# A new stored order and new engine choices for the same pieces of an attention and spatial-gate kernel

## The chip, the cores and the metric

The kernel runs on one core of one Trainium2 chip. The core has a matrix engine (TensorE, "PE" in the profile, with its weight loads as "PEld"), three engines for elementwise work (VectorE "DVE", ScalarE "ACT", GpSimd "POOL"), a queue engine that issues DMAs (SyncE "SP") and 16 DMA engines. Each engine runs its own instructions in their order and waits on semaphores for the others. The metric is the device time of one execution in microseconds, the median of several runs.

## The reference

Batch 8, 8 heads, 576 positions, head size 64. Two attentions are added: one over positions pooled by 4, one over a band of 7 positions. Their sum x, with the heads joined, goes through a gated MLP whose gate mixes positions.

```python
q_d = q.reshape(B, H, Sd, factor, D).mean(axis=3)      # k_d, v_d likewise
out_up = np.repeat(sm_attn(q_d, k_d, v_d), factor, axis=2)
mask = np.abs(pos[:, None] - pos[None, :]) < factor
out_local = softmax(np.where(mask, scale * q @ k.T, -1e9)) @ v
x = out_up + out_local                                  # (8, 576, 512)
h = gelu_tanh(x @ w_in)                                 # 512 -> 1024
u, v = h[..., :512], h[..., 512:]
v_n = (v - mu) / np.sqrt(var + 1e-06) * g_ln            # over the last axis
v_s = np.einsum('ts,bsd->btd', w_sg, v_n) + b_sg[None, :, None]
out = x + (u * v_s) @ w_out
```

## The kernel before

The work is 32 groups g = 0 to 31 (a batch and a pair of heads; four groups make a batch) and 8 MLPs (a batch each). All of it is cut into 2105 named pieces ("tasks"), each on one engine. Nothing is scheduled on the way: the string ORDER (lines 88 to 195) lists the names, and `place` (line 64) and the last loop of the kernel emit the pieces one after another in that order. A name may carry an engine (`/V` VectorE, `/A` ScalarE, `/P` GpSimd, `/S` SyncE); otherwise its piece has one engine. So ORDER sets the sequence of every engine's instructions, SyncE's loads among them, and also which buffer a piece gets: a pool of 8 PSUM banks, 10 buffers "X" and 38 buffers "R" are handed out first freed, first taken.

```python
for word in ORDER.split():
    name, _, e = word.partition("/")
    t = named.pop(name)
    for k in t.takes:
        where[k] = free[k[0]].pop(0)
    for k in t.gives:
        readers[k] -= 1
        if not readers[k]:
            free[k[0]].append(where[k])
    order.append((t, e or next(iter(t.engines))))
```

The names, with the group or the batch and piece as number:

- Loads on SP: lq, lk (q and k of a group, 293 KB each), lv (v in groups of four, for the pooled attention), lw (v in windows), w.. (weights), small and b (constants). os stores a quarter of a batch's output.
- qs, ks: pooled sums of q and k (line 391 on VectorE, 394 and 395 on GpSimd); vs the same of v, on GpSimd, from group 4 on.
- S and Y, or YS: scores of the band and of the pooled attention on TensorE (lines 417, 424, 445). Groups 0 to 3 have them as two pieces.
- ma, mb, mx, my, nx, ny: mask, row maxima and biases. ea, eb, ec: exponentials on ScalarE (lines 484, 492). re, rc: sums and reciprocals. np, nq: the normalization of both (lines 506, 509).
- T, U, t: transposes of the probabilities on TensorE (lines 512, 521). pa, pb, pc, pe: their evacuation from PSUM (line 221).
- D: probabilities by v on TensorE (lines 573, 589). oe, od, xa, xb: upsampling and sum of both attentions, on VectorE for the most part. xh, xl, xc: x split into a high and a low part.
- v (vk in batch 0, where the piece is cut in four): x by the half of w_in that is gated by position (line 691, 512 columns). vg, va, vj: GELU. vb, vp, vn: layer norm. vh, vl: high and low part.
- u, ua: the other half of w_in (line 769) and its GELU on ScalarE (line 788).
- s: the spatial product (line 769); sa, sm: bias (line 807) and gate (line 814); gh, gl: high and low part.
- o (ok in batch 7): w_out (line 769); oa adds x (line 843).
- wu, wq, wb, wt, wh, wl: the weights, which come as 64-bit numbers, are turned into a high and a low float32 part (lines 299 to 326).

Weights and activations stand in two parts each, and three products of the parts are added, so v, u, s and o are runs of 8 to 14 matmuls of 288 or 512 columns ("wide" work). S, Y, YS and D are many matmuls of at most 64 x 64 weights, several of them in different quarters of the array at a time. A YS leaves 56 matmul records in the trace, a D 56 (104 in groups 0 to 3), each with a weight load.

Of the kernel before, what the change touches and what calls it, by code (L numbers as in the profile page):

```python
# [98 lines left out]
od3 xa3 xb3 vk0.2 ea5 xc2 vk3.2 T4 wtr2 wlz1/V eb5 xh3/A re5/V rc5 nq5/P wq3 t4 np5/P U4 vk4.2 vk2.2 wq2 pa4/A xl3/V  # L99
v0.0 xc3 lq8 wuz0 wqr1/A ks6/V wtz0 wbr1 pb4/V pc4/V pe4/A v0.2 vg0.2 vb0.2 wq0 lk7 ks7/V vg0.0 vb0.0 v0.3 vg0.3 wr3  # L100
lw4 wtr1 v0.1 vg0.1 whz0/A wlz0/P v0.4 va0.4/A whz3/A whq3/A vj0.4 vg0.4 whq0/A vp0.2 wlz3/P whr2/A YS6 ma6 mb6 my6
wlq0/P D4 lq7 vb0.1 vp0.1 T5 pa5/A vp0.0 oe4/A od4 lw6 ks8/V qs7/P whq2/A vn0.2 u0.0 xa4 u0.1 ua0.0 ua0.1 vn0.1 vb0.4
vp0.4 lv5 u0.4 ua0.4 wur3 wq4 vh0.1/A whq4/A vh0.2/A wqr0/A wur0 u0.5 ua0.5 U5 vn0.0 mx6 vb0.3 xb4 wlq3/P vh0.0/A
pb5/A vn0.4 u0.6 vp0.3 vn0.3 wlr2/V whq1/A wlq1/V pc5/A ua0.6 vh0.3/A t5 pe5/A wqr3/A lq9 lk10 vh0.4/A u0.2 ua0.2 u0.3
vl0.2/V vl0.0/V ny6/A wlq4/V wlq2/V vl0.1/V lv6 lq15 lw5 nx6/V qs8/V YS7 ma7 ua0.3 u0.7 ua0.7 vl0.3/P vl0.4/V mb7 wbr0
vs6 vs5 mx7 s0.1 sa0.1 ea6 sm0.1/P lk11 my7 eb6 lq13 lw8 ny7/A ec6 s0.0 sa0.0 sm0.0/V wbr3 wtr3 s0.3 re6/V sa0.3
sm0.3/P wtr0 s0.2 sa0.2 xh4/A rc6 np6/V nx7/A ec7 qs9/V YS8 gh0.0/A gl0.0/V ma8 mb8 mx8 eb7 sm0.2/V nq6/P whr3/A
wlr3/P D5 oe5/A T6 pa6/A gh0.1/A ea7 s0.5 sa0.5 lw7 sm0.5/P lk9 ks9/V s0.4 sa0.4 od5 my8 ny8/V gl0.1/V s0.6 t6 U6
re7/A whr1/A pb6/A lq10 s0.7 lw13 lv8 lw9 sm0.4/P sa0.6 lq14 lk14 gh0.2/A pc6/A pe6/A nx8/V xa5 rc7 ec8 sa0.7 sm0.7/V
sm0.6/P YS9 xb5 wlr1/P D6 ea8 gh0.3/A whr0/V gl0.2/P gl0.3/V o0.6 o0.7 my9 oe6/V ma9 mb9 od6 xa6 xb6 eb8 mx9 re8/A rc8  # L110
xh5/A o0.4 xl5/V oa0.4 lv7 lq12 lq11 wlr0/P o0.0 oa0.0 ks10/P np7/P T7 xh6/A ny9/A nq7/P U7 pa7/V pb7/V pc7/A t7 pe7/V
oa0.6 oa0.7 o0.1 oa0.1 os0.0 nx9/A ea9 ec9 qs10/P YS10 my10 ny10/A eb9 re9/A vs7 D7 oe7/V od7 ma10 mb10 mx10 nx10/A
eb10 qs11/V xa7 rc9 xb7 xh7/V np8/P T8 lk12 lv13 nq8/P o0.2 t8 xl4/P xl6/P xc6 oa0.2 xl7/P lv9 ks11/V o0.3 pa8/V U8
pb8/A ea10 ec10 re10/V rc10 v1.1 vg1.1 vb1.1 v1.0 pc8/A vg1.0 YS11 pe8/V vs8 D8 oa0.3 ma11 mb11 mx11 nq9/P xc7 nq10/P
np9/P U9 oe8/V nx11/V ea11 T9 pa9/V od8 vb1.0 xa8 eb11 lw12 lk13 my11 v1.2 u1.4 ny11/A vg1.2 pb9/V pc9/A vs9 o0.5
np10/P vb1.2 vp1.0 vn1.0 vh1.0/V T10 lv10 ks12/P qs12/P xc5 xc4 vl1.0/V vp1.1 vn1.1 vp1.2 ua1.4 vn1.2 t9 pe9/A U10
ec11 re11/V v1.4 va1.4/A vj1.4 vg1.4 xb8 pa10/V pb10/A vb1.4 u1.2 ua1.2 v1.3 vg1.3 rc11 vh1.2/V lk16 YS12 my12 os0.1
ma12 oa0.5 mb12 D9 vb1.3 oe9/V t10 ny12/V ec12 lw11 lw10 os0.2 nq11/P vp1.4 od9 xa9 xb9 np11/P mx12 u1.5 ua1.5 vp1.3
vn1.3 pc10/V pe10/V vs10 ks13/P os0.3 vh1.3/A vh1.1/A u1.6 ua1.6 qs13/V vl1.2/V u1.7 ua1.7 u1.3 ua1.3 D10 vn1.4
vh1.4/V vl1.4/P vl1.1/P lq19 lv11 YS13 ma13 mb13 nx12/A ea12 vl1.3/P ks14/V my13 oe10/V eb12 T11 lv12 vs12 vs11 U11  # L120
u1.0 od10 xa10 xb10 mx13 xh10/A xl10/P nx13/A ny13/A pa11/A eb13 pb11/A s1.1 sa1.1 t11 pc11/A ec13 pe11/A s1.3 re12/V
rc12 nq12/V np12/V s1.0 sa1.0 qs14/P ua1.0 u1.1 ua1.1 s1.2 YS14 ma14 mb14 mx14 xh8/A xh9/A xl9/P nx14/V eb14 sm1.0/P
sa1.2 sm1.2/P D11 oe11/V sm1.1/V sa1.3 gh1.0/A sm1.3/V T12 od11 pa12/V s1.7 my14 ny14/A ea14 s1.5 sa1.5 xa11 xb11 s1.4
lv14 xc10 t12 sm1.5/P xl8/V ea13 xh11/V sa1.7 xl11/V xc11 vs13 U12 pb12/A pc12/V s1.6 re13/A rc13 np13/V v2.0 ks16/P
v2.3 gl1.0/P xc9 ec14 re14/A rc14 vg2.0 lk15 ks15/V T13 sm1.7/V nq13/V np14/P pa13/V U13 pb13/A pe12/A vg2.3 pc13/V
t13 u2.4 ua2.4 gh1.1/A qs15/V lk19 sa1.4 YS15 ma15 mb15 D12 pe13/V T14 u2.5 my15 ny15/A ec15 oe12/V gl1.1/V v2.1 vg2.1
pa14/V mx15 sm1.4/P sa1.6 sm1.6/P nx15/V vb2.0 lq16 qs16/V gh1.3/V vp2.0 vn2.0 gl1.3/V od12 xa12 xb12 gh1.2/A gl1.2/P
v2.2 vg2.2 u2.2 vb2.3 vp2.3 xc8 vb2.1 vp2.1 YS16 ma16 mb16 D13 oe13/V nq14/V vn2.3 eb15 ea15 ua2.2 re15/A rc15 nq15/P
# [5 lines left out]
eb17 od15 xa15 xb15 xh15/A xl15/P ua2.1 lv17 lk18 my17 ks18/V s2.0 sa2.0 sm2.0/V sa2.1 lq18 qs18/P ny17/V sm2.1/V u2.6
s2.2 sa2.2 lv16 sm2.2/V ua2.6 xh12/A ea17 lk21 u2.7 xl13/P xc13 s2.3 sa2.3 sm2.3/V vs16 s2.5 sa2.5 ec17 sm2.5/V s2.6
xl12/P lk23 xh14/A xl14/P ua2.7 s2.4 gh2.1/A sa2.4 sm2.4/V sa2.6 sm2.6/P U16 YS18 ma18 mb18 mx18 T16 pa16/V t16
gh2.2/A xc15 gl2.2/P my18 ny18/V ec18 s2.7 sa2.7 sm2.7/V lk20 pb16/V pc16/V re17/A gh2.3/A v3.0 u3.0 ua3.0 vg3.0 vb3.0
pe16/A v3.1 vg3.1 lw21 gl2.3/P gl2.1/P v3.2 os1.1 nx18/V rc17 nq17/P vp3.0 np17/V gh2.0/A vg3.2 vb3.1 YS19 my19 ma19
mb19 mx19 D16 eb18 ea18 oe16/A od16 xa16 re18/V rc18 gl2.0/P vs17 T17 pa17/A U17 pb17/V pc17/A v3.3 vg3.3 vp3.1 u3.5
nq18/P vb3.2 o2.6 xb16 oa2.6 o2.2 oa2.2 o2.0 vn3.1 vh3.1/A vn3.0 t17 np18/P T18 pa18/A u3.4 vb3.3 o2.3 vp3.2 oa2.3  # L140
pe17/V vn3.2 vp3.3 ua3.4 nx19/A ea19 o2.1 ks20/V lw17 os2.1 vh3.0/V lq20 vn3.3 oa2.0 oa2.1 qs20/V xc14 xc12 v3.4
va3.4/V o2.4 oa2.4 o2.7 oa2.7 U18 o2.5 ny19/A ua3.5 ec19 u3.6 pb18/V vj3.4 vg3.4 vb3.4 pc18/V oa2.5 YS20 ma20 my20 D17
t18 ua3.6 vp3.4 vn3.4 vh3.4/V u3.1 vl3.0/V u3.2 mb20 vh3.2/A pe18/V lw18 mx20 vl3.2/V qs21/V vh3.3/A lk22 ny20/A eb19
# [845 lines left out]
```

## Time and profile before

| | us |
|---|---|
| median of 3 runs | 574.63 |
| lowest and highest run | 574.22, 578.1 |
| the profiled execution | 574.64 |
| its span, first to last instruction | 572.9 |
| busy: TensorE matmuls, weight loads | 552.4, 517.2 |
| busy: VectorE, ScalarE, GpSimd | 407.7, 356.6, 320.8 |

The granted TensorE clock is 1.000 in the whole span. TensorE's matmuls are 6992 and cover 96% of the span, but "busy" counts from a matmul's start to its modelled end, and consecutive matmuls overlap; how far apart they start tells their cost better. The three elementwise engines are idle 29% to 44% of the time. The loads (52.64 MB read in all) come mostly in the first tenth of the span, when the weights are read and prepared too. Instruction fetches are DMAs as well; the page has them as queues of kind "instruction". In a list of waits, "issue" stands where an engine was idle and the profile shows nothing that it waited for.

### The profile page before, as it was taken

How to read it: one execution, taken by the hardware profiler on the slowest of the kernel's cores; microseconds unless marked ns; L12 is line 12 of the kernel's file. 1: busy time of each engine (PE TensorE's matmuls, PEld its weight loads, DVE VectorE, ACT ScalarE, POOL GpSimd, SP SyncE). 2: the span in 40 equal slices, each digit the busy share in tenths (PEclk: the TensorE clock that was granted, in tenths of full speed). 3: DMA queues.
4: the chain of work that ended last, by engine and by line, in shares of the span. 5: the costliest groups of instructions: out<-in, count | busy, mean ns of one | idle time of the engine just before them, and what ended most of it. 6: DMA issues, size and time to landing. Idle time of an engine off the chain costs nothing. (4 is left out here: it accounts for less than half of the span.)

```text
span 572.9 us, 17455 instructions
## 1 busy us (share of the span) xinstructions
PE 552.4 (96%) x6992; PEld 517.2 (90%) x6992; DVE 407.7 (71%) x912; ACT 356.6 (62%) x1236; POOL 320.8 (56%) x403
## 2 busy tenths in 40 slices
PE   5689999999999999999998999999999999999997
...
GB/s 312 299 305 363 60 242 154 115 81 153 78 61 23 122 107 150 88 2 67 203 107 94 105 63 262 26 120 25 1 108 141 57 15 53 2 1 1 64 1 185
DMA packets 30609, 63.21 MB, mean 110 GB/s; under 512 B 3520, under 2 KB 3776, under 8 KB 30528
## 3 DMA queue, kind: packets, MB, share of 16 engines
...
q8 instruction: 55, 0.90, 0.7%
q10 hardware_dynamic: 144, 0.30, 0.1%
...
HBM read 52.64 MB, written 9.44 MB: 108 GB/s over the span
## 5 line engine op out<-in xcount | busy, mean ns | idle before, releaser
L769 PE MATMUL ps<-wsg_h,R 128*128 128x288 f32 x576 | 121.4, 298 | 0.1
L769 PE MATMUL ps<-X,weight_z 128*128 128x288 f32 x512 | 109.0, 297 | 0.5 <-ACT pd L492 0.5
L769 PE MATMUL ps<-R,weight_r 128*128 128x288 f32 x768 | 107.4, 296 | 0.0
L769 PEld LDWEIGHTS ps<-R,weight_r 128*128 128x128 f32 x768 | 103.1, 188 | 0.5 <-ACT R L788 0.2
L691 PE MATMUL ps<-weight_y,X 128*128 128x512 f32 x320 | 97.8, 399 | 0.0
L484 ACT ACTIVATE X<-X,nb 128x64 f32<-128x64 f32 x280 | 93.6, 339 | 5.7 <-DVE nb L463 5.4
L769 PEld LDWEIGHTS ps<-wsg_h,R 128*128 128x128 f32 x576 | 93.9, 188 | 0.6 <-issue 0.4
L769 PE MATMUL ps<-wsg_l,R 128*128 128x288 f32 x320 | 92.5, 295 | 0.0
L769 PEld LDWEIGHTS ps<-X,weight_z 128*128 128x128 f32 x512 | 84.2, 188 | 1.5 <-ACT pd L492 0.7
L769 PE MATMUL ps<-R,weight_z 128*128 128x288 f32 x256 | 75.5, 295 | 0.0
L691 PEld LDWEIGHTS ps<-weight_y,X 128*128 128x128 f32 x320 | 57.9, 188 | 11.3
L769 PEld LDWEIGHTS ps<-wsg_l,R 128*128 128x128 f32 x320 | 60.2, 188 | 0.0
L807 DVE SCALAR_TENSOR_TENSOR vs<-ps,small_sb,b_sb 128x288 f32<-128x288 f32 x64 | 32.5, 512 | 38.1 <-PE ps L769 35.4
L814 POOL TENSOR_TENSOR R<-R,vs 128x288 f32<-128x288 f32 x34 | 28.6, 848 | 54.7 <-DVE vs L807 30.4
L221 ACT COPY R<-ps 112x192 f32<-112x192 f32 (+4 forms) x74 | 28.1, 395 | 45.8 <-PE ps L512 14.4
L732 POOL TENSOR_TENSOR rs<-rs,nhalf 128x1 f32<-128x1 f32 (+1 forms) x40 | 23.9, 599 | 56.7 <-DVE rs L723 54.3
L484 ACT ACTIVATION_READ_ACCUMULATOR X<-X,nb 128x1 f32 x280 | 53.3, 190 | 0.0
L221 ACT CAST R<-R 128x576 fp32r<-128x576 f32 (+2 forms) x46 | 29.5, 648 | 36.0 <-DVE R L814 15.1
L691 PE MATMUL ps<-weight_y,R 128*128 128x512 f32 x128 | 50.5, 394 | 0.0
L843 DVE TENSOR_TENSOR R<-ps,R 128x288 f32<-128x288 f32 x64 | 27.8, 450 | 30.2 <-PE ps L769 30.2
L760 POOL TENSOR_TENSOR R<-R,R 128x512 fp32r<-128x512 f32 (+1 forms) x24 | 32.2, 1349 | 30.0 <-DVE R L221 14.9
L769 PEld LDWEIGHTS ps<-R,weight_z 128*128 128x128 f32 x256 | 48.2, 188 | 0.7
...
## 6 DMA issues: line engine op xcount, KB each, us to landing
...
```

The source lines that it names most:

```text
L221: (nc.scalar.copy if e == "A" else ENG[e].tensor_copy)(**kw)
L484: nc.scalar.activation(out=st["ms"][:, t, :], in_=src, func=AF.Exp, bias=st["nb"][:, t:t + 1], scale=scale, accum_out=sums[par][:, t:t + 1])
L691: nc.tensor.matmul(out=acc, lhsT=r32(l), rhs=r32(weights[f"y{k}"][:, 0, w]), start=(i == 0 and ks[0] == 0), stop=(i == len(ops) - 1 and ks ...
L732: nc.gpsimd.tensor_tensor(out=rs[0:n], in0=rs[0:n], in1=nhalf[0:n], op=ALU.pow)
L760: ENG[e].tensor_tensor(out=r32(dst), in0=vact[s][0][0:n], in1=vh[0:n, 0:DM], op=ALU.subtract)
L769: nc.tensor.matmul(out=acc[:, 0:HALF], lhsT=r32(l), rhs=r32(r), start=(first and n == 0), stop=(last and n == len(ops) - 1))
L807: nc.vector.scalar_tensor_tensor(out=vsb[i], in0=at["ps", "m", b, "s", i][:, 0:HALF], scalar=g_sb[:, i // 2:i // 2 + 1], in1=b_sb[:, half( ...
L814: ENG[e].tensor_tensor(out=u[:, half(i)], in0=u[:, half(i)], in1=vsb[i], op=ALU.mult)
L843: nc.vector.tensor_tensor(out=x[:, half(i)], in0=at["ps", "m", b, "o", i][:, 0:HALF], in1=x[:, half(i)], op=ALU.add)
```

## The change

Only the string ORDER is replaced. It holds the same 2105 names. Their sequence is new on every engine and on SP's queue, and where a piece may run on one of two engines the choice differs for some: of the evacuations pa, pb, pc, pe 88 of 128 are now on ScalarE (68 before), of oe 19 of 32 (10 before); of gh 15 of 32 are on VectorE (8), of xh 18 of 32 (10), of sm 39 of 64 (30), the rest of sm being on GpSimd; qs and ks move between VectorE and GpSimd, with GpSimd's share of the two going from 26 to 29 of 64. No piece changes what it computes, and the pools keep their sizes. Cut to the start, the places where YS and D pieces stand side by side, and the end:

```diff
-lk0/A lq0/S ks0/P qs0/V Y0 my0 ny0/V ec0 small wy1 lq1/S qs1/P wqy1/V wby1 wuy1 wy0 wuy0 wqy0/A S0 mx0 lk1/S S1 ks1/P
-wby0 nx0/A ea0 eb0 re0/A mx1 lq2 qs2/V wty1 lk2 wz1 wuz1 wty0 ks2/P Y1 my1 nx1/V rc0 ea1 ny1/V S2 ec1 mx2 np0/P wy3
-wqy3/V nq0/V T0 why0/V wly0/P t0 U0 pa0/V pb0/V pc0/V pe0/V Y2 my2 wqz1/V nx2/A eb1 re1/V why1/V rc1 np1/P nq1/P lk4
-lw0/S lv0/S wz2 lq4 wbz1 wuz2 wqz2/A D0 wby3 ny2/A lk6 lq3 ea2 oe0/V od0 xa0 ks4/V qs3/V lk3 wuy3 lv1/S wty3 wly1/P
-qs4/P T1 eb2 ks3/P xb0 pa1/V wtz1 lw1/S S3 mx3 ec2 re2/A rc2 xh0/A why3/A nq2/V nx3/A U1 ea3 YS4 ma4 lv3 mb4 wy2 t1
-pb1/A my4 pc1/V pe1/A eb3 Y3 my3 ny3/A ec3 ny4/A wbz2 whz1/V xl0/P xc0 D1 t2 mx4 lv2 np2/P T2 re3/A U2 oe1/V wqy2/A
-pa2/A wtz2 vk3.0 rc3 nq3/P np3/P ec4 od1 xa1 xb1 xh1/A vk0.0 lk5 ks5/V pb2/V vk1.0 lq5 qs5/V pc2/A pe2/A wby2 YS5 wz3
-whz2/A lw2 xl1/P xc1 wr0 wr1 nx4/A vk0.1 vk3.1 wuy2 wq1 ma5 mb5 mx5 my5 D2 wqz3/A wbz3 ea4 wty2 why2/A eb4 ny5/A lv4
-oe2/V od2 xa2 wz0 xb2 vk1.1 T3 wr2 wur1 nx5/A lw3 re4/V U3 pa3/A pb3/A wlz2/P wly3/P pc3/V lq6 xh2/A wuz3 rc4 xl2/V t3
-pe3/V vk2.0 wly2/P vk4.0 vs4 nq4/P np4/P vk2.1 wqz0/A wbz0 vk1.2 lk8 qs6/V vk4.1 ec5 wtz3 b wur2 wqr2/A wbr2 D3 oe3/V
...
-pb14/V os1.2 vl2.0/P lq21 lw15 os1.3 vh2.1/A vl2.1/P ea16 vn2.4 u2.3 ua2.3 u2.0 ua2.0 qs17/V os1.0 vh2.4/V pc14/V YS17
-ma17 qs19/P pe14/A re16/A D14 mb17 mx17 oe14/A od14 vl2.4/V xa14 xb14 rc16 nq16/V D15 ks19/V oe15/V np16/V s2.1 nx17/A
...
-s3.5 YS21 T19 t19 re20/V my21 sa3.5 ma21 ny21/A rc20 U19 ec21 s3.7 pa19/V pb19/V pc19/A pe19/A ks22/V YS22 os2.3 D18
-oe18/A sm3.5/V gl3.1/P np20/P gh3.2/V gl3.2/P sa3.7 sm3.7/P ma22 mb22 lw19 D19 mb21 nq20/V T20 mx21 pa20/V od18 oe19/V
...
-oa3.3 va4.4/A vj4.4 u4.6 ua4.6 u4.4 ua4.4 vp4.1 vn4.1 vh4.1/V vl4.0/P YS23 my23 vl4.1/P ny23/V ma23 mb23 vg4.4 vb4.4
-mx23 vp4.4 D20 oe20/V ec23 D21 od20 oe21/V od21 xa20 U22 pb22/V xb20 xa21 xb21 u4.7 vs22 nx23/A ea23 eb23 u4.1 ua4.1
...
-s7.5 sa7.5 o6.7 sm7.5/P gh7.2/A s7.6 s7.7 sa7.7 sm7.7/V sa7.6 sm7.6/V oa6.6 oa6.7 os6.3 os4.3 os6.0 os6.2 gl7.2/P ok3
-ok2 ok1 ok0 gh7.3/A gl7.3/V o7.2 oa7.2 o7.3 oa7.3 os7.1 o7.0 oa7.0 o7.1 oa7.1 o7.4 oa7.4 o7.6 oa7.6 os7.3.0 os6.1 o7.5
-oa7.5 os7.2 os7.0 o7.7 oa7.7 os7.3.1
+lk0/A lq0/S ks0/V qs0/V Y0 my0 ny0/A small S0 ec0 wy1 wuy1 lq1/S qs1/P wqy1/V wby1 wty1 mx0 wy0 lk1/S S1 ks1/P wqy0/A
+wby0 lk2 ks2/V mx1 lq2 qs2/P lq3 Y1 S2 my1 wuy0 wy3 wqy3/V nx0/A ea0 eb0 re0/V rc0 qs3/P ny1/V nx1/A ea1 wby3 mx2 ec1
+np0/P T0 nq0/P pa0/V U0 pb0/V pc0/V t0 pe0/V wz1 Y2 wty0 lk3 why1/V wqz1/V eb1 re1/V rc1 lk5 nq1/P wuz1 nx2/V ea2
+lw0/S lv0/S D0 oe0/A eb2 my2 ny2/V lq5 wbz1 np1/P U1 T1 why0/V wly0/P ks3/V od0 xa0 ec2 lk4 ks4/V t1 pa1/A pb1/A wuy3
+lw1/S lq4 qs4/V wtz1 whz1/V wlz1/P wz2 pc1/A pe1/V Y3 my3 wy2 wqz2/A xb0 re2/A rc2 np2/P S3 mx3 ny3/A ec3 qs5/V lv1/S
+wz3 nx3/A ea3 YS4 my4 ma4 ny4/A nq2/P wty3 wly1/P mb4 T2 pa2/A eb3 ks5/V wbz2 xh0/V U2 pb2/A xl0/P re3/A rc3 nq3/P lw2
+pc2/V np3/P t2 pe2/A lv2 lv3 D1 oe1/V od1 xc0 xa1 YS5 ma5 mb5 xb1 wuz2 wtz2 lv4 wqy2/A ec4 wqz3/A vk0.0 vk2.0 wby2 T3
+wuy2 wty2 my5 why3/A pa3/A xh1/A U3 pb3/A t3 wuz3 mx4 xl1/V nx4/V wly3/V ny5/A pc3/A pe3/V wr0 ec5 D2 oe2/A vs4 wz0
+wbz3 xc1 lk6 od2 xa2 xb2 mx5 vk2.1 wq0 lw3 lw8 wq4 xh2/V eb4 vk1.0 whz2/A ea4 re4/V vk4.0 vk3.0 vk1.1 wtz3 whz3/A
+why2/V whq0/A wuz0 wqz0/A vk4.1 vk0.1 nx5/A eb5 wly2/V wr2 D3 xl2/V vk1.2 vk2.2 vk0.2 xc2 wr1 lq6 rc4 nq4/P np4/P wq3
+vk3.1 ks6/V lq7 oe3/V od3 xa3 xb3 wlz3/V xh3/V ea5 re5/A xl3/P xc3 wlq0/P vk4.2 vk3.2 T4 wbz0 wtz0 U4 whq4/A t4 wlq4/V
+v0.0 v0.2 rc5 qs6/V wqr2/A pa4/A wbr2 nq5/P wq2 lw4 vg0.0 vb0.0 v0.4 vp0.0 lw5 wlz2/P pb4/A lw13 qs7/V pc4/A va0.4/A
+vj0.4 b wq1 pe4/A v0.1 whz0/A vg0.1 vb0.1 vp0.1 u0.6 vn0.0 wlz0/P lv6 wr3 wqr0/A v0.3 whq3/A vg0.3 vb0.3 vg0.2 vg0.4
...
+vl1.1/P pc11/V pe11/V vp1.2 vn1.2 ua1.7 u1.1 ua1.4 ua1.5 vh1.2/V ks13/P YS13 my13 ma13 mb13 vl1.4/V lq14 D11 D10
...
+vb2.0 pb13/V pc13/V t13 pe13/V lk16 ks16/V YS15 pe12/A vp2.0 my15 ma15 ny15/V ec15 lv14 D12 oe12/V od12 mb15 mx15
+nx15/A vb2.2 eb15 D13 oe13/V xa12 od13 vp2.2 vs14 os0.3 v2.4 va2.4/A o1.6 rc14 o1.2 o1.0 ea15 vn2.2 oa1.6 vn2.0
...
+sa2.3 xb14 u2.7 lq21 lw21 s2.4 ua2.7 lw17 os1.2 sm2.2/P sa2.4 sm2.4/V mx17 sm2.3/V s2.5 sa2.5 YS18 ma18 mb18 my18 D15
+oe15/A od15 nx17/A xh14/V eb17 xa15 xb15 U16 t16 s2.7 ea17 sm2.5/P qs19/P xc12 sa2.7 xh15/V xl14/P xl15/V v3.0 vg3.0
...
+pa28/A YS30 ma30 os4.2 os4.3 sm5.7/P gh5.3/V gl5.3/P D26 oe26/A od26 xa26 gl5.2/V xb26 xh26/V xl26/P D27 oe27/A U28
...
+oa5.1 t29 pe29/V eb30 YS31 ma31 D28 vs30 vn6.3 mb31 mx31 os5.1 os5.0 nx31/A eb31 oe28/V od28 vn6.2 vh6.2/V xa28 D29
...
+sm7.3/P gh7.1/A gl7.1/P s7.7 sa7.5 sm7.5/V s7.4 sa7.4 sm7.4/V s7.6 sa7.6 sa7.7 sm7.6/V gh7.2/V gl7.0/P o6.0 u7.7 ua7.7
+gl7.2/V ok2 ok0 sm7.7/V gh7.3/V gl7.3/V ok1 o7.0 oa7.0 o7.2 oa7.2 oa6.0 oa6.1 os6.1 o7.6 ok3 oa7.6 os5.2 os6.0 o7.1
+oa7.1 o7.4 o7.5 os7.0 os7.3.0 oa7.4 oa7.5 os7.2 o7.3 oa7.3 os7.1 o7.7 oa7.7 os7.3.1
```

More of the change, by code (lines that the diff above doesn't have):

```diff
@@ L99 @@
[L99 to L128, printed above, removed]
@@ L134 @@
[L134 to L143, printed above, removed]
@@ L174 @@
-pc28/A D26 oe26/V od26 ea29 D27 oe27/A gh5.3/V gl5.3/P xl24/P xa26 xb26 YS30 my30 ma30 t28 ny30/A ec30 od27 xh26/V
-xa27 xb27 xh27/A xl26/P xl27/V o5.2 o5.3 mb30 mx30 lv28 qs31/V nx30/V lk31 ks31/V v6.0 re29/A pe28/A rc29 nq29/V vg6.0
-vb6.0 np29/P vs29 eb30 vs28 v6.2 vg6.2 vb6.2 u6.0 ua6.0 v6.1 oa5.2 oa5.3 os5.1 xc27 T29 U29 pa29/A vp6.2 vn6.2 pb29/A
-pc29/V D28 vg6.1 YS31 ma31 mb31 vh6.2/A vl6.2/P ea30 re30/A vp6.0 vn6.0 vh6.0/V vb6.1 t29 pe29/V v6.3 vg6.3 u6.1 ua6.1
-lw29 D29 oe28/V od28 oe29/A u6.6 ua6.6 mx31 xc25 od29 xc24 xa29 vp6.1 vn6.1 my31 nx31/A ny31/A vl6.0/P xc26 vb6.3 v6.4
```

121 lines of the change are left out of this document (81 added, 40 removed).

## The prediction

> **What bounds the kernel.** I read the page's busy shares and slices first, then a table by stage, then TensorE's waits by stage, then the timeline at each pause.
>
> ```profile
> span 572.9 us, 17455 instructions
> PE 552.4 (96%) x6992; PEld 517.2 (90%) x6992; DVE 407.7 (71%) x912; ACT 356.6 (62%) x1236; POOL 320.8 (56%) x403
> PE   5689999999999999999998999999999999999997
> q8 instruction: 55, 0.90, 0.7%
> ```
> ```profile
> core 0: us, PE busy (x) PEld busy (x) DVE busy (x) ACT busy (x) POOL busy (x), PEclk, DMA share, GB/s
> 299.91:302.17 2.26, 2.26 (x140) 2.26 (x136) 1.83 (x6) 0.29 (x1) 2.09 (x2) 1.00 0.91 252
> 338.22:340.48 2.26, 2.26 (x141) 2.26 (x137) 1.82 (x6) 1.55 (x3) 1.26 (x1) 1.00 0.06 10
> 213.36:216.08 2.72, 2.72 (x144) 2.66 (x134) 2.19 (x5) 0.76 (x4) 2.53 (x4) 1.00 0.10 23
> 39.60:45.70 6.10, 5.93 (x132) 4.90 (x127) 5.34 (x13) 5.57 (x26) 5.79 (x6) 1.00 1.04 311
> 6.10:62.20 56.10, 48.71 (x991) 38.82 (x991) 49.20 (x112) 50.38 (x211) 44.10 (x48) 1.00 0.96 306
> 62.20:569.50 507.30, 503.67 (x6004) 478.36 (x6002) 356.89 (x797) 306.22 (x1026) 274.47 (x347) 1.00 0.28 87
> 569.50:572.90 3.40, 0.00 (x0) 0.00 (x0) 0.42 (x1) 0.00 (x0) 0.00 (x0) 1.00 0.50 184
> ```
>
> TensorE is the bound. From 62.2 us on it is idle 507.30 - 503.67 = 3.6 us; in the start (6.1 to 62.2) 56.10 - 48.71 = 7.4 us; 6.1 us lie before its first matmul and 3.4 behind its last. The matmuls are the same in both kernels, so an order can win only from these, and from what TensorE pays when it changes between kinds of work.
>
> ```profile
> PE ps L589 <- issue: 2.6, 2, 1.8
> PE ps L769 <- ACT pd L492: 0.5, 1, 0.5
> PE ps L445 <- ACT R L788: 0.3, 1, 0.3
> ...
> PEld ps L445 <- issue: 1.8, 10, 0.4
> ```
> ```profile
> 46.85 0.35 PE L521 MATMUL ps<-small_sb,pd 112*112 112x112 f32 x2 [0.90 <-PE ps L521]
> 216.49 0.30 PEld L769 LDWEIGHTS ps<-wsg_h,R 128*128 128x128 f32 x2 [0.36 <-issue]
> 304.16 0.57 PE L589 MATMUL ps<-R,X 64*64 64x58 f32 x24 [1.77 <-issue]
> 341.55 0.57 PE L589 MATMUL ps<-R,X 64*64 64x58 f32 x23 [0.86 <-issue]
> ```
>
> Of the 3.6 us idle after the start, 2.6 are two pauses in which no engine is waited for. They are instruction fetches. Queue q8 moved 55 pieces of 0.90 MB / 55 = 16 KB, and TensorE issued 2 x 6992 = 13984 instructions: 254 a piece. Counted from TensorE's first instruction, waits included, the four pauses above stand at numbers 1473, 6337, 8385 and 9153: each is 193 above a multiple of 256. The block ahead of each was used up in 2.26, 2.26, 2.72 and 6.10 us (rows above; 140 + 136 of them, less those that lie over an edge). From a block's first instruction to the first of the next, pause included, it took 304.16 - 299.91 = 4.25, 341.55 - 338.22 = 3.33, 216.49 - 213.36 = 3.13, and with the loads at 311 GB/s 46.85 - 39.60 = 7.25 us. I read this as: the next block is asked for when one is entered, arrives 3.1 to 4.25 us later (up to 7.25 under the loads of the start), and TensorE stops if the block is used up sooner. Only bursts of small matmuls do that: YS (56 matmul records), a late D (56), an early D (104). Here are YS22 D18 D19, YS23 D20 D21 and YS17 D14 D15.
>
> [...]
>
> **The change, part by part.** Only the string ORDER differs: each engine's sequence and some choices of engine; the 415 TensorE tasks are the same.
>
> *Late fetch pauses.* Three D/YS in a row stand in the new order four times: YS13 D11 D10, YS15 D12 D13, YS30 D26 D27, YS31 D28 D29. With two instructions a matmul and the waits spread as before, the block edge falls 220, 124, 179 and 125 instructions into bursts of about 340. So a block holds at most 220 instructions of a burst and at least 36 of wide work. Wide matmuls go every 0.13 us:
>
> ```profile
> 299.00 0.29 PE L769 MATMUL ps<-wsg_l,R 128*128 128x288 f32 x1
> ...
> 299.13 0.30 PE L769 MATMUL ps<-wsg_h,R 128*128 128x288 f32 x1
> ```
>
> The shortest block then lasts 2.26 x 220/276 + 18 x 0.13 = 4.1 us, near the upper turnaround of 4.25, and before it the queue could run ahead through the wide work. I take no pause. Gain: 1.77 + 0.86 + 0.36 = **-3.0 us**. If the waits are spread otherwise the edges move by a dozen instructions, which leaves that.
>
> *The start.* I walked the new lists of the five queues by hand to the end of v0.3 (the last v of batch 0), each task at its duration in the trace, starting when its engine is free and its inputs are there.
>
> ```profile
> 4.80 0.75 DVE L391 TENSOR_REDUCE qd<-R 128x144 f32<-128x576 f32 x1 [3.60 <-DMA R<-in_qT_dram]
> ...
> 4.96 0.66 POOL L394 TENSOR_TENSOR half<-R 128x288 f32<-128x288 f32 x1 [3.28 <-DMA R<-in_kT_dram]
> ...
> 6.19 1.33 PE L445 MATMUL ps<-kd,qd 64*64 64x144 f32 x16 [6.19 <-POOL kd L395]
> ...
> 8.51 1.28 ACT L492 ACT_TABLE_LOAD   x1 [8.51 <-DVE nbd L475]
> ...
> 16.67 1.26 POOL L506 TENSOR_TENSOR X<-X,rc 128x640 f32<-128x640 f32 x1
> ...
> 17.98 0.64 PE L512 MATMUL ps<-small_sb,X 122*128 122x122 f32 x4 [2.00 <-POOL X L506]
> ...
> 35.73 0.91 POOL L509 TENSOR_TENSOR pd<-pd,rc 128x432 f32<-128x432 f32 x1
> ...
> 37.82 1.42 POOL L608 TENSOR_TENSOR R<-R,X 128x576 fp32r<-128x576 f32 x1
> ```
>
> ks0 goes to VectorE ahead of qs0: 4.96 + 0.66 + 0.75 = 6.4, Y0 0.2 later. ny0 goes to ScalarE ahead of ec0: 0.2 later; if the table loaded for it isn't that of exp, 1.28 more. Then np0 (1.26) starts at 16.9 to 17.4 instead of 16.67, because re0 and rc0 now stand behind wqy3 on VectorE: T0 at 18.2 to 18.7 instead of 17.98. U1 and T1 wait for np1 until 24.4 to 25.0. But t1 and Y3 follow without the old gaps, and YS4 is done at 29.5 to 30.0, with the same work behind it that was done at 31.45. T2 then waits for np2 until 31.8 to 32.4. T3 waits for GpSimd, which has xl0, nq3 and np3 in a row from 36.0: 1.42 + 0.91 + 1.26, so 39.6 to 40.2; t3 is done at 40.6 to 41.1, against 40.1 for the same work before. From there D2, D3 and the v pieces find their inputs, and v0.3 ends at 59.6 to 60.2. Before, TensorE began u0.0 at 62.2, with YS6, D4 and T5 behind it (2.65 us) but u0.6 (1.6) not; that makes 61.1. So 0.9 to 1.5 sooner, the old pause at 46.85 counted in. On SP's queue lq3, lk3 and lk5 go ahead of lv0 in place of lk4: two loads of 0.3 MB, 1.9 us at 311 GB/s. D0, which waited for evacuations and not for lv0, is itself 0.5 to 1 us later; if lv0 ended last, about 1 us is lost there.
>
> Against that stand the new order's own pauses in the start. D1 and YS5 are now next to each other, with the edge 78 instructions into D1: that block (130 instructions of D1, YS5, vk0.0) takes some 3.4 us. Turnaround there: 5.8 to 7.25. The pause is 2.4 to 3.9, but T3 has 2 us of its own waiting behind it, so 1.3 net, and 0.4 for the next block (5.9 us). Bounds: 0 (the fetch is early) to 5.2 (3.9 + 1.3, nothing absorbed). Sum for the start: -1.2 + 1.7 = **+0.5**.
>
> *Changes between kinds of work.* From wide work to a burst: 27 before, 21 after; from transposes (T, U, t) to a burst 8 and 12; transpose to other transpose 37 and 45; burst to anything else 36 and 34. None costs over 0.18 us (1.8 over 10, in the row of TensorE's weight-load waits above); by the start-to-start times of each kind, -0.5 + 0.6 + 0.6 - 0.3 = **+0.4**.
>
> *Engine choices.* 20 evacuations (pa to pe) more on ScalarE, 9 sm from GpSimd to VectorE, 7 gh from ScalarE to VectorE, 10 changes of ScalarE's table fewer (56 to 46).
>
> ```profile
> L814 POOL TENSOR_TENSOR R<-R,vs 128x288 f32<-128x288 f32 x34 | 28.6, 848 | 54.7 <-DVE vs L807 30.4
> ...
> L484 ACT ACT_TABLE_LOAD x18 | 23.1, 1283 | 0.3
> ```
>
> GpSimd loses about 14 us, ScalarE 10 x 1.28 = 13, VectorE stays. All are idle at least 28% of the time, and TensorE's queue covers them: **0**. Without that cover a place costs what one late operation does, 0.5 to 0.85. Known old waits in the later part are 0.5 + 0.3; I find some six more close places in the new order than in the old (D15 stands 2.4 us ahead of v3.0, with od15, xa15, xb15, sa2.7, xh15, xl15 between on VectorE), most covered because the late operand comes last in the accumulation: **+0.3**, from -0.8 to +4.
>
> *The end.* Behind s7.6 come o6.0, u7.7, ok2, ok0, ok1 (51 wide matmuls at 0.13, 6.6 us) while VectorE finishes gl7.2 and gl7.3; last are o7.7, its add and a half store as before: 3.4 us stay. **0**.
>
> Sum, against the profiled execution's 574.64 (span 572.9 and 1.7 around it; the median of the runs is 574.63): 574.6 - 3.0 + 0.5 + 0.4 + 0.3 = **572.8**, say 572.6.
>
> **The rivals.**
> *Faster still.* The walk is too careful about the start; half of its 7.4 us of idle time goes and the early fetch is hidden: 574.6 - 3.0 - 3.7 + 0.4 = 568.3. For it: VectorE and ScalarE idle there too. Against: four norms in a row gate T0 to T3.
> *Slower: the fetch moves into the start.* The block of D1 and YS5 is asked for while the loads run (311 GB/s), and nothing absorbs the pause: 574.6 - 3.0 + (5.2 - 1.2) + 0.4 + 0.3 = 576.3. It decides once the pauses in the start exceed some 3.5 us. For it: the 7.25 row. Against: T3's wait lies behind.
> *The pauses aren't fetches,* and come in bursts wherever they stand; the start then has none of its own: 574.6 + 0.4 + 0.3 with -1.2 to +0.5 for the start, 575.0. Against: the four numbers. [...]
> *New waits in the later part,* at the joins D to v and s to o: +4, 576.3. Against: counted in TensorE's work, the median distance from the last v of a batch to its first s goes from 13.6 to 16.5 us and from the last s to the first o from 3.9 to 5.6; only that from the last D to the first v or u shrinks, 8.3 to 6.7.
>
> **How the numbers follow.** Forecast 0.46 (570.5 to 574.5 by the bounds of the start and of the waits), faster still 0.2, slower by the fetch 0.14, not fetches 0.08, new waits 0.12. The range 567.5 to 577.5 leaves out the outer half of the first rival and the tails of the others, 2 in 10. One per cent, about what a measurement of this kernel can tell from none, is 5.7 us: under 568.9 lies a little over half of the first rival with a tail of the forecast, 0.16; over 580.4 only tails of the slower ones, 0.06; 0.78 between.
>
> **What would show it.** Right: no idle time of over 0.5 us with "issue" inside a burst after 62 us, and a stage from 62 us that is busy to within 2 us; T0 at about 18.5; T1 at 24.5; a pause near YS5 to T3 at 37 to 41. Wrong: a pause of 1 us or more at any of the four triples (the reach of a block is then misread); the start shorter or longer than 56 us by over 3; many waits of VectorE's or ScalarE's making at v or o.

## The result and the profile after

The kernel after takes 572.49 us (median of 19 runs, 571.23 to 575.65). The kernel before, run beside it, takes 575.92 (19 runs, 574.22 to 578.56). The ratio is 0.994, 95% interval 0.9924 to 0.9956: about 3.4 us, within 1%. The two profiled executions, 574.64 and 573.11 us, differ by only 1.5. Part of why the medians differ by more is found below, under the clock.

The page of the kernel after, its span, busy times and TensorE's slices:

```profile
span 571.3 us, 17427 instructions
PE 553.5 (97%) x6992; PEld 517.8 (91%) x6992; DVE 412.9 (72%) x908; ACT 342.6 (60%) x1242; POOL 312.8 (55%) x394
PE   5899999999999999999899999999999999999997
```

The span is 1.6 us shorter, TensorE's busy time 1.1 us longer, so its idle time fell by 2.7 us, from 20.5 to 17.8. The table by stage of the kernel after says where (columns as in the prediction; its last matmul ends at 567.9):

```profile
6.10:62.20 56.10, 50.45 (x908) 40.76 (x909) 51.03 (x116) 49.85 (x214) 42.30 (x46) 1.00 0.95 313
62.20:567.90 505.70, 503.05 (x6086) 477.00 (x6084) 359.93 (x788) 291.42 (x1028) 269.31 (x342) 1.00 0.28 87
```

In the start TensorE is idle 56.10 - 50.45 = 5.65 us instead of 7.4; from 62.2 us to its last matmul 2.65 instead of 3.6; behind that 3.4 us as before. So 1.75 us come from the start, where a loss of 0.5 was forecast, and 1.0 from the later part, where 2.7 were (3.0 of pauses less 0.3 of new waits). TensorE's waits in the later part of the kernel after say what took the rest:

```profile
PE ps L769 <- DVE R L596: 1.7, 1, 1.7
PE ps L573 <- ACT R L788: 0.4, 1, 0.4
PE ps L512 <- ACT R L788: 0.3, 1, 0.3
```

No row with "issue" is left: the two pauses that made up 2.6 us are gone. In their place stands one wait of 1.7 us for VectorE. The timeline around it (start, duration, engine, line, operation; in brackets the idle time ahead and what ended it):

```profile
271.83 0.36 SPq L848 DMA_DIRECT2D out_dram<-R  x1
276.43 0.46 DVE L596 TENSOR_TENSOR R<-ps,od 128x290 f32<-128x290 f32 x1 [3.15 <-DMA out_dram<-R]
276.94 2.26 PE L769 MATMUL ps<-R,weight_r 128*128 128x288 f32 x15 [1.73 <-DVE R L596]
```

Read it from the bottom. The matmuls of o2.2 need the PSUM bank that xa17 (line 596) empties. xa17 stood still for 3.15 us, not for data, but for a buffer: ORDER hands it the "R" buffer out of which the store os2.2 is being read, and that store, issued at 271.83, lands 4.5 us later. So a store holds up TensorE by way of VectorE; in the kernel before no row of the waits names a store.

In the start one fetch pause is left, at TensorE's instruction number 1473 as before, now inside vk1.1:

```profile
45.56 0.39 PE L691 MATMUL ps<-weight_y,R 128*128 128x512 f32 x1 [1.14 <-issue]
```

The start differs from one execution to the next. In a second profile of the kernel after, taken for the question of the clock below, TensorE is idle 4.91 us there instead of 5.65; no pause stands at number 1473, one of 0.35 us stands at 705, and D0 waits 0.57 us for lv0. Over the profiles of this document the start is idle 4.5 to 5.65 us in five that begin as the kernel after does, and 7.4 and 6.4 in two that begin as the kernel before does (the second has two windows at half clock there). So the sign of the change in the start is safe, its size only to about 1 us.

### The profile page after: what moved, and what is told of

It reads as the page before. It is cut to its first block, busy times and chain, and to the rows that moved or that the text cites. A ratio compares the mean times of both kernels' runs of the same rounds, so it can differ in the third digit from the quotient of the medians.

```text
span 571.3 us, 17427 instructions
## 1 busy us (share of the span) xinstructions
PE 553.5 (97%) x6992; PEld 517.8 (91%) x6992; DVE 412.9 (72%) x908; ACT 342.6 (60%) x1242; POOL 312.8 (55%) x394
## 4 chain that ended last, share of the span: by engine, by line
PE 84%; DVE 5%; ACT 2%; issue 1%; DMA 1%; POOL 0%; DVEq 0%; ACTq 0%
PE ps L769 52%; PE ps L691 17%; PE ps L589 3%; PE ps L512 3%; PE ps L445 3%; PE ps L573 2%; PE ps L521 2%; PE ps L424 2%; DMA out_dram<-R 1%; DVE R L740 1%; DVE st L721 1%; DVE R L760 1%; DVE X L432 0%; DVE stats L456 0%; ACT R L221 0%
## 5 line engine op out<-in xcount | busy, mean ns | idle before, releaser
L769 PE MATMUL ps<-X,weight_z 128*128 128x288 f32 x512 | 110.2, 297 | 0.0
L814 POOL TENSOR_TENSOR R<-R,vs 128x288 f32<-128x288 f32 x25 | 22.0, 880 | 51.6 <-DVE vs L807 33.8
L408 POOL TENSOR_TENSOR pairs<-R 112x256 f32<-112x256 f32 x56 | 45.4, 811 | 7.2 <-DMA R<-in_v_dram 7.0
L221 ACT COPY R<-ps 128x464 f32<-128x464 f32 (+4 forms) x92 | 33.8, 407 | 25.7 <-PE ps L512 13.9
L788 ACT ACTIVATE R<-ps 128x288 f32<-128x288 f32 x64 | 24.8, 410 | 40.1 <-PE ps L769 38.3
L221 ACT CAST R<-R 128x512 fp32r<-128x512 f32 (+2 forms) x38 | 24.5, 647 | 35.3 <-DVE R L814 12.6
```

The source lines that it names most:

```text
L221: (nc.scalar.copy if e == "A" else ENG[e].tensor_copy)(**kw)
L408: ENG[e].tensor_tensor(out=pairs, in0=v[:, 0:2], in1=v[:, 2:4], op=ALU.add)
L769: nc.tensor.matmul(out=acc[:, 0:HALF], lhsT=r32(l), rhs=r32(r), start=(first and n == 0), stop=(last and n == len(ops) - 1))
L788: nc.scalar.activation(out=us[i // 2][:, half(i)], in_=at["ps", "m", b, "u", i][:, 0:HALF], func=AF.Gelu_apprx_tanh)
L814: ENG[e].tensor_tensor(out=u[:, half(i)], in0=u[:, half(i)], in1=vsb[i], op=ALU.mult)
```

## The experiments

**Do the pauses follow the instruction numbers?** Small matmuls ahead of all work, each four TensorE instructions, move every later number and nothing else in ORDER:

```diff
+ warm = psum.tile([P, 512], F32, name="ps0")
+ for _ in range(22):            # 64, and 32 on the kernel before
+     nc.tensor.matmul(out=warm[0:HD, 0:HD], lhsT=od2[0][0:HD, 0:HD],
+                      rhs=od2[0][0:HD, HD:2 * HD], start=True, stop=True)
```

22 on the kernel after:

> The kernel after, with 22 small matmuls (88 TensorE instructions) put ahead of everything, in time in which TensorE waits for its first operands. Nothing else changes, but every later instruction has a number 88 higher, so the 256-instruction edges fall elsewhere: 132 instead of 220 instructions into the triple YS13 D11 D10, 36 instead of 124 into YS15 D12 D13, 91 instead of 179 into YS30 D26 D27, 37 instead of 125 into YS31 D28 D29. Theory (the pauses are instruction fetches; a block that is used up in under about 3.3 us makes TensorE wait): a pause of 1 to 2 us without a releaser near the end of the second block at YS15 D12 D13 and at YS31 D28 D29, 0 to 0.9 us at YS30 D26 D27, none at YS13 D11 D10; the pause at 44 us in the start moves to another place or goes. Time 2 to 4 us longer than the kernel after if the start stays. Rival (the pauses come in bursts for another reason, and the new order has cured that): no pause at any of the four, time as the kernel after within 1 us.

TensorE's pauses with "issue" in the start and in the later part, from the timeline of this kernel:

```profile
26.80 0.27 PE L512 MATMUL ps<-small_sb,X 122*128 122x122 f32 x1 [2.08 <-issue]
35.50 0.50 PE L521 MATMUL ps<-small_sb,pd 112*112 112x112 f32 x3 [2.56 <-issue]
46.59 0.69 PE L589 MATMUL ps<-R,X 64*64 64x58 f32 x31 [0.48 <-issue]
192.42 0.56 PE L589 MATMUL ps<-R,X 64*64 64x58 f32 x19 [0.61 <-issue]
465.63 0.46 PE L589 MATMUL ps<-R,X 64*64 64x58 f32 x17 [0.39 <-issue]
```

They stand at numbers 705, 961, 1473, 5569 and 12481, each 193 above a multiple of 256. The two late ones are in YS15 D12 D13 and YS31 D28 D29, the triples that the theory named, and none is in YS13 D11 D10 or YS30 D26 D27. The place is right and the size too large: 0.61 and 0.39 us idle instead of 1 to 2. The block ahead of the one at 192.42 was used up in 2.22 us, and from its first instruction (189.38) to the next block's it took 3.04 us, so the turnaround is a little under the 3.1 to 4.25 read from the kernel before.

The traces also hold the fetches themselves, as packets of queue q8. In each of the pauses named so far of the kernels before and after, one piece of q8 lands 1.2 to 1.5 us before TensorE goes on: 1.5, 1.2 and 1.3 us in the late pauses of the kernel before (1.77, 0.86 and 0.36 us), 1.3 in its pause at 46.85 us, 1.4 in the one of the kernel after at 45.56. So these pauses end with a fetch. In the late ones the piece starts 0.7 to 1.8 us after the block ahead is entered, in the two of the start 4.9 and 6.1 us after it, which is why pauses come there in blocks that last 6 to 7 us.

The time, 580.73 us (ratio to before 1.0058, interval 1.004 to 1.0076), is 8 us above the median of the kernel after, which was measured apart from it; the late pauses don't explain that. The profiled execution, 577.57 us, is the fastest of the twelve. In it the two pauses of over 2 us in the start are the larger part, and they have a sequel:

```profile
32.98:36.39 3.41, 0.89 (x19) 0.74 (x23) 2.32 (x5) 2.25 (x16) 2.42 (x3) 1.00 0.52 131
36.39:39.81 3.42, 3.42 (x103) 3.42 (x95) 0.41 (x2) 3.42 (x12) 3.42 (x5) 0.50 0.79 243
39.81:43.22 3.41, 2.98 (x71) 2.56 (x66) 3.10 (x8) 0.45 (x1) 0.39 (x1) 1.00 0.90 285
```

In the table by stage PEclk, third from the end, is 0.50 for 3.41 us right behind a stretch in which TensorE was busy 0.89 of 3.41 us. All 12 executions of this kernel have a mean granted clock of 0.985 to 0.997.

64, the same edges again:

> Control for the run with 22 matmuls: 64 of them (256 instructions), so that every edge falls where it fell in the kernel after. Theory of fetches: the same places without pauses as in the kernel after, the pause at 44 us in the start again, time within 1 us of the kernel after. If the small matmuls themselves did something (a warmer TensorE, a queue held up), it shows here too: first matmuls of Y0 and S0 shorter, up to 1 us gained; or a first matmul later than 6.5 us, and as much lost.

Behind 62 us no pause with "issue" came back, and the wait for VectorE at o2.2 stayed (1.4 us): as the theory says of equal edges. In the start TensorE stood 1.1 us at number 1473 again, this time with VectorE named as its releaser. For the time it is no control: the 64 small matmuls keep TensorE busy from 1.47 to 15.4 us, longer than it had to wait, so its first real matmul starts at 15.44 instead of 6.5, 8.9 us later, which is about what the 580.98 us (1.0058, 1.0045 to 1.0071) lie above the kernel after.

32, on the kernel before:

> The kernel before, with 32 small matmuls (128 TensorE instructions) ahead of everything. By the numbers the edge moves from 36 to 164 instructions into YS17 D14 D15 and YS22 D18 D19 , from 89 to 217 into YS23 D20 D21, and from 171 to 43 into D26 D27 YS30. Theory of fetches: the three late pauses of the kernel before (0.36, 1.77 and 0.86 us) go, the one at number 1473 in the start goes or moves, and a new one of 1 to 2 us comes in D26 D27 YS30; sum 1 to 2 us shorter. Rival (pauses belong to their bursts): the three stay where they were, none comes at D26 D27 YS30, time as the kernel before.

All three late pauses of the kernel before are gone. The one new pause stands where the theory put it, in D26 D27 YS30 at number 11969, and again smaller than said, as the timeline of this kernel shows:

```profile
442.05 0.56 PE L424 MATMUL ps<-R,R 64*64 64x64 f32 x20 [0.25 <-issue]
```

The time, 578.25 us (1.0031, 1.0012 to 1.0051), didn't fall: the first real matmul starts 2.5 us later here, and the pauses in the start moved too. So the rival is out for the places. What a pause costs depends on its place: 0.25 to 1.8 us behind 62 us, up to 2.6 in the start.

**The wait at o2.2.** The kernel after with one load moved, so that another buffer comes up for xa17:

```diff
-... o2.5 oa2.5 os2.2 lk25 vh3.3/A vl3.3/V od17 nq18/V xa17 o2.6 ...
+... o2.5 oa2.5 os2.2 vh3.3/A vl3.3/V od17 nq18/V xa17 lk25 o2.6 ...
```

> The kernel after with the load lk25 moved from ahead of od17 to behind xa17 in the stored order, so that xa17 no longer takes the buffer out of which the store os2.2 is still being read. Theory (o2.2 waited 1.73 us at 276.9 us for VectorE, and VectorE for that store to land): the wait of 1.7 to 2.0 us goes, no other comes within 10 us, time 1.5 to 2 us shorter than the kernel after. Rival (TensorE would have waited there anyway, for ScalarE or for another buffer): a wait of over 1 us stays at o2.2, or comes back within some 20 us, and the time is the same within 0.5 us.

TensorE's waits in its later part, and that part in the table by stage:

```profile
PE ps L573 <- ACT R L788: 0.4, 1, 0.4
PE ps L512 <- ACT R L788: 0.3, 1, 0.3
```
```profile
62.20:565.90 503.70, 502.64 (x6085) 476.80 (x6083) 358.13 (x788) 291.10 (x1028) 268.54 (x341) 1.00 0.28 87
```

The wait is gone and nothing took its place: 1.06 us of idle time are left of 2.65. 571.17 us (4 runs), ratio 0.9891 (0.9879 to 0.9904), an interval that doesn't meet that of the kernel after, though each was taken beside its own runs of the kernel before. The theory holds for the wait; the gain is priced further down, where the same edit stands beside the kernel after.

**The start and the rest apart.** The one order up to the last v piece of batch 0, then the other with what is left:

```diff
-ORDER = new
+ORDER = new up to v0.3, then old without those names
```

> The new order up to the last v of batch 0 (the start, to about 60 us), behind it the old order with what is left. Nothing is left out. In the two profiles TensorE had lost 18.8 us by the end of the start before and 17.4 after. Theory (the start gained 1.4 us, the gain behind it is the three fetch pauses less the new waits): this kernel has the start of the kernel after and the later part of the kernel before, with the edges at other numbers only where the order differs; 1 to 2 us shorter than the kernel before. Rival (the start gained nothing: the difference between the two profiles is the spread of the loads from run to run): the time of the kernel before within 0.7 us.

("Lost" there is a piece's start less what the pieces ahead of it take back to back.) 580.37 us, 1.0066 (1.0046 to 1.0087): neither theory. The trace says why. TensorE's instruction number 1473 starts at 45.43 us, in the kernel after at 45.56, so the start did what it does there. But at the seam the old order finds other work in VectorE's list and other buffers free than it was laid out for: D4 gets the PSUM bank out of which wbr1 (line 311, a part of w_out) still reads on VectorE until 62.51, and starts then. TensorE's waits in the later part:

```profile
PE ps L589 <- issue: 2.4, 2, 1.5
PE ps L573 <- DVE R L311: 2.0, 1, 2.0
PE ps L769 <- DVE R L826: 1.2, 1, 1.2
PE ps L769 <- DVE X L432: 0.9, 1, 0.9
PE ps L512 <- POOL X L506: 0.8, 1, 0.8
```

L573, L512 and L432 wait at 62.6, 64.6 and 66.2 us, at the seam, and TensorE's clock is at 0.50 from 65.2 to 72.0. The two old pauses (2.4) are there as well.

The other way round:

> The old order up to the last v of batch 0, behind it the new order with what is left. Theory (the start is worth 1.4 us, the later part 0.5 to 2): 0.5 to 2 us shorter than the kernel before, with no pause without a releaser behind 62 us and with the wait of 1.7 us at o2.2. Rival (all the gain is in the later part): as fast as the kernel after, within 0.7 us.

576.72 us, 1.0006 (0.9984 to 1.0028). Behind 62 us no pause without a releaser, as expected; but the 1.7 us at o2.2 didn't come, and two waits at the seam did (0.9 and 0.8 us for the parts of w_in). xa17 still gets the buffer that os2.2 reads, and still waits for it:

```profile
279.06 0.46 DVE L596 TENSOR_TENSOR R<-ps,od 128x290 f32<-128x290 f32 x1 [1.30 <-DMA out_dram<-R]
```

But VectorE waited 1.30 us for the store here and not 3.15, and TensorE had other matmuls for that long. So the shared buffer is a risk whose price depends on when the store lands: 1.7 us of TensorE's time in the kernel after, none here. The old start in this profile:

```profile
14.74:18.15 3.41, 1.57 (x44) 1.03 (x43) 3.41 (x11) 3.38 (x21) 3.04 (x4) 1.00 1.06 308
18.15:21.57 3.42, 3.42 (x35) 2.77 (x37) 2.41 (x7) 3.42 (x20) 1.27 (x1) 0.50 1.04 377
...
28.39:31.81 3.42, 1.90 (x65) 1.51 (x67) 3.32 (x9) 2.96 (x14) 3.19 (x5) 1.00 0.95 267
31.81:35.22 3.41, 3.41 (x66) 3.20 (x63) 3.19 (x8) 3.38 (x23) 3.35 (x5) 0.50 0.99 313
```

Twice TensorE is busy about half of 3.41 us (waiting for T0, and around YS4 to D1), and twice the next 3.41 us go at half the clock. The seams cost as much as the halves gain, so these two runs don't price the halves, and what the new start is worth by itself stays open; what they show is the half clock of the old start.

**Is the clock the order's or the chip's?** The kernel after, unchanged:

> The kernel after, unchanged, beside the kernel before and the two kernels below on one chip, with the granted clock of every execution. Theory (part of the gain is that the new start no longer has 3.4 us windows in which TensorE is nearly half idle, after which the clock is granted at one half for 3.4 us): all executions of the kernel after at 0.999 to 1.0, most of the kernel before at 0.997 or lower (one window is 1.7 us of 575, 0.003); ratio 0.991 to 0.996. Rival (the clock is the chip's and not the order's): both kernels show the same clocks.

572.63 us (10 runs), 0.9941 (0.9917 to 0.9966). Of 21 executions of the kernel before beside it, 14 have a mean granted clock of 0.997 or lower; of the kernel after 2 of 10. One window is 3.41 x 0.5 = 1.7 us, or 0.003 of the span: 0.997, 0.994 and 0.991 are one, two and three. The executions with a clock of 0.999 or 1.0 have medians of 574.52 (7, before) and 572.42 (8, after), 2.1 us apart. The other 14 of the kernel before have 577.3. So of the 4 us between these two medians about half is left at full clock, and the other half goes with the windows of half clock, which the new order seldom has. (The profile of the old start above shows such windows at 18 and 32 us, that of the kernel before none; where those of the other executions lie isn't recorded.) Mostly as the theory said; "all" was too much.

The clock isn't the whole spread, though. Over the 66 executions of the kernel before that stand beside the runs of this document the medians are 575.0 us at a clock of 0.999 or 1.0 (18), 575.9 with about one window by the clock (15), 577.3 with two (18) and 577.6 with three (15): about 0.9 us a window, not 1.7. And the 18 at full clock lie between 573.64 and 577.55; the 19 first executions of the kernel after have 0.999 or 1.0, all of them, and lie between 571.23 and 575.65. Where these 4 us come from no run settles.

**Order and engines.** The new order with the old engine letters (312 of 718 differ: oe0/A becomes oe0/V, sm3.0/V becomes sm3.0/P), and the old order with the new ones:

```diff
-each name at its place, with its own engine letter
+each name at its place, with the other kernel's letter
```

> The new order with the old choices of engine for each of its pieces. Theory (the choices are worth nothing, because the engines are idle at least 28% of the time and TensorE is the bound): within 1 us of the kernel after. Rival (order and choices were found together, and the order needs them: ScalarE loads its table more often, GpSimd has 9 more slow operations): new waits of TensorE for VectorE, ScalarE and GpSimd, 2 us or more longer than the kernel after.

> The old order with the new choices of engine. Theory: within 1 us of the kernel before. Rival (the choices are themselves the gain: fewer table loads, a lighter GpSimd): 1.5 us or more shorter than the kernel before.

631.46 us, 1.0955 (1.0926 to 1.0985), and 639.27 us, 1.1075 (1.1036 to 1.1114). My theory fell by an order of magnitude, and the rival of the second fell with it: neither set of choices suits the other's order. Table loads of ScalarE, which both rivals named, go with the order: 46 in both kernels of the new one, 56 in both of the old. The first of 29 rows of TensorE's waits in the later part of the first:

```profile
PE ps L512 <- POOL X L506: 3.8, 3, 2.2
PE ps L521 <- POOL pd L509: 3.2, 1, 3.2
PE ps L445 <- DVE kd L391: 2.2, 2, 1.7
PE ps L521 <- DVE R L311: 1.9, 1, 1.9
PE ps L445 <- ACT R L703: 1.9, 1, 1.9
```
```profile
6.00:62.20 56.20, 43.99 (x845) 34.19 (x846) 39.26 (x91) 41.34 (x190) 34.48 (x40) 0.94 0.90 283
62.20:626.00 563.80, 527.75 (x6149) 491.88 (x6147) 375.18 (x817) 303.20 (x1038) 286.56 (x355) 0.99 0.26 81
```

The engines' busy time hardly changed (VectorE 415.6, ScalarE 344.5, GpSimd 323.2 in all), yet TensorE is idle 36 us behind 62.2 us, for all three engines, at many places, and it loses clock besides (0.94 in the start).

A part of the choices, the 33 of the sm pieces:

```diff
-sm3.0/V ... sm3.2/V ... sm2.0/P
+sm3.0/P ... sm3.2/P ... sm2.0/V
```

> The new order with the 33 choices of engine for the pieces named sm set back to the old ones (21 from VectorE to GpSimd, 12 the other way); the other 279 changed choices stay new. Theory A (a choice matters by its place in the in-order queue of the engine: the 312 choices together cost 57 us with the new order): about a tenth of that, 3 to 9 us longer than the kernel after, as new waits of TensorE at s, v and o. Theory B (only the load of each engine counts, and it has room): within 1 us. Theory C (the 57 us come from few critical places, none among these): within 1 us, with no new waits.

576.35 us, 3.7 more than the kernel after beside it, so theory A by size. The waits behind 62 us of this kernel:

```profile
PE ps L512 <- POOL X L506: 1.7, 1, 1.7
PE ps L769 <- DVE R L596: 1.3, 1, 1.3
PE ps L521 <- DVE X L432: 0.6, 1, 0.6
```

Not at s, v and o, as I had said: the first is at T20, for which np20 (line 506) starts on GpSimd at 299.44 instead of 296.16 in the kernel after, some 2 us more than everything there is late. A gate piece (line 814, 0.79 us) now runs on GpSimd ahead of it. The price fell on what stood behind that piece in GpSimd's list. The waits are only part of the price: against the second profile of the kernel after the span is 4.1 us longer, of which idle time behind 62 us makes 2.3, while TensorE's busy time is 2.2 longer, and what stretches that no run shows.

**Further.** The wait at o2.2 taken out, and ua3.4 moved up ahead of a table load:

```diff
-... ny19/V ec19 xb16 o2.4 xc13 u3.4 mx19 nx19/A ua3.4 ks20/P ...
+... ny19/V xb16 o2.4 xc13 u3.4 ua3.4 ec19 mx19 nx19/A ks20/P ...
```

> The kernel after with lk25 behind xa17, as tried before, and with ua3.4 moved up to stand right behind u3.4 on ScalarE, with ec19 behind it. Theory: the wait of 1.7 us at o2.2 is gone as before; ua3.4 no longer stands behind a load of ScalarE's table and two other pieces, so the waits for ScalarE at 264 to 267 us (0.4 and 0.3 us by the row, 0.9 us by the start of T18) go too; 2.3 to 2.9 us shorter than the kernel after in this call. Rival: the 0.9 us at T18 stays because another operand is late there; 1.5 to 2.1 us shorter.

570.60 us (6 runs), 0.9911 (0.9878 to 0.9944), 2.0 less than the kernel after beside it. The 0.4 us of L573 for ScalarE are gone, but a new 0.4 has come, u3.3 for VectorE:

```profile
PE ps L769 <- DVE X L432: 0.4, 1, 0.4
PE ps L512 <- ACT R L788: 0.3, 1, 0.3
```

So the second edit gave back what it won; the first is the gain.

To that, two weight loads later:

```diff
-... pe3/V wr0 ec5 ...   ... xc2 wr1 lq6 ...   ... vk3.2 T4 wbz0 ...
+... pe3/V ec5 ...       ... xc2 lq6 ...       ... vk3.2 T4 wr1 wr0 wbz0 ...
```

> The kernel of the run above, with the loads wr0 and wr1 (two weight loads of 512 KB, used only behind batch 0's first v pieces) moved from about 36 and 40 us in SyncE's list to behind T4 (about 48 us). Theory (the fetch of the block that is entered at 37 us started only at 43.2 us because some ten loads stood before it in the same DMA engines): with 1 MB less before it, it starts 2 to 3 us sooner, the pause at TensorE's instruction number 1473 falls from 0.9 to 1.5 us to under 0.5, and the time is up to 1 us shorter than that of the run above. Rival (the fetch is late for another reason): the pause stays; or wr0 and wr1 now come late for ScalarE and GpSimd and the waits move to the stage from 55 us.

570.52 us, 0.99 (0.9872 to 0.9929): no difference. There was nothing left to cure: the pause at number 1473 had not come in the run above either (no row with "issue" among TensorE's waits up to 62 us in either). The edit didn't do what it was meant to: the loads behind wr0 moved up, so SyncE's queue was as full as before, 11 loads issued between 36 and 44 us against 10 there. Why the fetch for that block came as late as it did in the kernel after, 6.1 us behind the block's entry, is not settled.

## Why the prediction was right, and where it wasn't

The forecast was 572.6, and the median is 572.49. Step by step it came out less well: the start was forecast 2.25 us too long and the later waits 1.7 too short, and the two cancel. That the sum met the median so closely is luck; that the late pauses go is not.

- *Late fetch pauses, -3.0*: right. All are gone, and none came at the four triples. The shifted kernels and the landings of q8 show that they are fetches.
- *The start, +0.5*: wrong sign. Its idle time fell by 1.75 us, with a pause of 1.14 in it, so by 2.9 without. The term that failed is the walk by hand (-1.2): T0 came at 17.69 (said 18.2 to 18.7), U1 at 23.35 (24.4 to 25.0), T2 at 29.68 (31.8 to 32.4), T3 at 37.06 (39.6 to 40.2). GpSimd's norms, on which I had the transposes wait, were earlier by 0.5 to 3 us: these are their starts in the kernel after, with the idle time of GpSimd ahead of the first.

```profile
16.37 1.26 POOL L506 TENSOR_TENSOR X<-X,rc 128x640 f32<-128x640 f32 x1 [0.79 <-DVE nbd L475]
22.04 1.26 POOL L506 TENSOR_TENSOR X<-X,rc 128x640 f32<-128x640 f32 x1
28.37 1.26 POOL L506 TENSOR_TENSOR X<-X,rc 128x640 f32<-128x640 f32 x1
35.74 1.27 POOL L506 TENSOR_TENSOR X<-X,rc 128x640 f32<-128x640 f32 x1
```

  The start's own pause (+1.7 in all) came at 1.14, in the block behind the one I named; the block of D1 and YS5 had its fetch 0.7 us after it was entered and didn't pause. Of the turnaround of 5.8 to 7.25 us that I took for it, 7.25 has its row, and no run shows the 5.8: in the kernel after the block with the pause took 8.4 us (37.12 to 45.56). The wait of D0 for lv0, which I had as a possibility, didn't come in this execution, but 0.57 us of it came in the second profile of the kernel after.
- *New late waits, +0.3 (-0.8 to +4)*: mis-sized. With 3.6 us of idle time before, 3.0 of it gone and 2.6 left, the waits grew by 2.0. 1.7 of it is xa17's wait for a store, and a wait of that kind I had not looked for: I had gone through late operands and not through who gets which buffer.
- *Changes between kinds of work, +0.4*: TensorE's busy time rose by 1.1 us. What of it is this term no run separates. "None costs over 0.18" misread its row: 0.18 is the mean of ten waits there, the longest is 0.4.
- *Engine choices, 0*: a term that can't be priced by itself, and the reason given for it is wrong. Idle engines don't make the choices free: with the other's choices the new order takes 59 us more than the median of the kernel after, the old one 63 more than the kernel before. The 10 table loads fewer belong to the order.
- *The end, 0*: right, 3.4 us.
- *Of the rivals* "the pauses aren't fetches" is out, by their places and by the landings. "New waits in the later part" came about by half. "Slower: the fetch moves into the start" didn't come, but the order shifted by 88 instructions is its case: over 5 us of pauses there.

The sum was made against one execution whose clock was full throughout, and holds against such: 574.52 to 572.42 is -2.1, against -1.8 in the sum. That most executions of the kernel before also lose one to three windows of half clock couldn't be seen in that execution, and it goes with about half of the difference between the medians.
